# A new order for the first thirty microseconds of an mLSTM and two-layer feed-forward kernel

## The chip, the cores and the metric

The kernel runs on one core of a Trainium2 chip. The metric is the device time of one execution in microseconds (us), the median of several runs.

## The reference, cut to what matters

An mLSTM over 2 batches, 8 heads, 768 steps and 40 features per head gives 1536 rows of 320 numbers; two feed-forward layers follow (widths 768 and 2048).

```python
for t in range(S):
    m_new = np.maximum(f_gate[:, :, t] + m, i_gate[:, :, t])
    f_stab = np.exp(f_gate[:, :, t] + m - m_new)
    i_stab = np.exp(i_gate[:, :, t] - m_new)
    C = f_stab * C + i_stab * outer(v_t, k_t)
    n = f_stab * n + i_stab * k_t
    y[:, :, t] = sigmoid(o_t) * (C @ q_t) / max(abs(n . q_t), 1)
x = y as (B*S, H*D)
h = maximum(maximum(x @ w1, x @ w2), x @ w3); x = h @ w_out
h = x @ w_in; g = h * tanh(softplus(h)); out = g @ w_out2
```

## The kernel before, in words

The sequence is cut into 6 chunks of 128 steps; with 2 batches that makes 12 units, u = 0 to 11. Units 0 and 1 are the first chunk of each batch, units 2 and 3 the second. The three products of the first layer are made in blocks of 512 rows, and the first block needs units 0 to 3 whole. So the beginning of the kernel is: gates, units 0 to 3, and then the first products.

The order of the work is written out by hand in PLAN (lines 31 to 65), a list of words. Each word is the name of a step, its arguments and, behind an @, the PSUM banks that it uses. follow (L660) goes through the words, and under manual_schedule (L671) each engine's queue gets its instructions in the order of the words. PE, DVE, ACT, POOL and SP have one queue each and work through it strictly in order; SP issues all transfers. Between engines only the data and the reuse of buffers and banks make one wait for the other. So a word that is moved changes its place on its own engine's queue and leaves the other queues as they were.

The words that matter here, with their engine and line:

- SP: first:0 to first:3 (L186) load the gates of the first chunk, the other gates, the identity idt and a mask; lq:u (L300, two transfers) loads queries and keys of a unit into qall, which has two buffers; ln:u (L305) loads na (values, keys, output gate of a unit, two buffers); l3:u (L310) another layout of the queries; out:c (L290, L294, L295) writes decays to DRAM, and lc:u (L330, three transfers) reads them back as broadcasts, cp; fet:w,g (L494) fetches group g of the nine groups of first-layer weights, with three buffers.
- DVE: ma (L191, L195), fa:0, ia:0, fl:0 and ca (L283) are the gates' scans; D:u,j (L346) makes half of a unit's decay matrix out of PSUM; X:u,j (L365) multiplies the scores into it; den (L405 to L407), xn (L418) and sg:2, sg:3 (L412) divide and gate; mg:w,g (L509) puts weights together.
- ACT: fe, ie (L210 to L217, L241, L243) are exponentials, pick (L267) and eye (L271) copy parts of idt, fl:1 (L224), gc (L260, L263), dl (L154), G (L386, a sigmoid), sc:w,g (L503, L504, two passes over a fetched weight group), rd (L154), C:0, C:1 (L478), sd (L468), xc (L154), xh (L441, L445). Changing between exponential and sigmoid costs a load of ACT's table.
- POOL: clear:4 to clear:7 (L171 to L178), fa, ia, flp (L204, L205, L236, L228), V (L371), K (L381), Q (L376), sg:0, sg:1 (L412), cut:w,g (L549, L551, L552).
- PE: fill:n (L487) makes n matmuls on zeros that nobody reads; F:u,j (L339) broadcasts decays into PSUM; S:u (L359) makes the scores; gt (L252, L255) transposes gates; N (L396, L398) makes a unit's output, O (L460) its state update, T (L429) transposes it; Pa and P (L578) are the products of the first layer.

## Time and profile before

| | us |
|---|---|
| median of 3 runs | 375.26 (375.0 to 375.54) |
| the profiled execution, its own time | 374.55 |
| span of the profiled execution, first to last instruction | 372.8 |
| PE busy in the span | 367.4 |
| DVE, ACT, POOL busy | 198.6, 175.5, 100.1 |
| moved by DMA | 38.80 MB, mean 104 GB/s |

The time lies 1.75 us above the span, which is what stands around the first and the last instruction. Busy time of PE is nearly the whole span, but it tells little of the beginning: there PE is often filled with matmuls that wait in a row behind the slowest of their suppliers.

### The profile page before, as it was taken

The page shows a single profiled execution, that of the slowest core. Times are in us where ns is not written, and L with a number is a line of the kernel's source. Part 1 is how long each engine was busy: PE and PEld are TensorE (multiplying, and loading weights), DVE is VectorE, ACT ScalarE, POOL GpSimd, SP SyncE. Part 2 cuts the span into 40 slices and gives each one's busy share as a digit, 9 for nine tenths or more (in the row PEclk, how much of TensorE's full clock was granted, in tenths as well). Part 3 has the DMA queues.
Part 4 walks back from the last instruction along what each step waited for, and adds up shares of the span by engine and source line. Part 5 has one row for each costly group of instructions (what it writes and reads, how often), then busy time and mean ns, then how long its engine had stood idle before and what let it go on. Part 6 is the DMA issues. An engine that isn't in the chain of part 4 may idle for free.

```text
span 372.8 us, 7435 instructions
## 1 busy us (share of the span) xinstructions
PE 367.4 (99%) x2999; PEld 317.2 (85%) x3000; DVE 198.6 (53%) x344; ACT 175.5 (47%) x353; POOL 100.1 (27%) x111
## 2 busy tenths in 40 slices
PE   8999999999999999999999999999999999999996
PEld 4898888888888898888777889989989989989986
DVE  6989999998556853565581745512212112212112
ACT  4887777933413202555644876543333233333231
POOL 6784575755202022311540052330010110000000
PEclk9999999999999999999999999999999999999999
DMA  7879995938590310033220530000200000200001
GB/s 204 270 248 307 355 283 166 267 100 273 192 316 8 105 55 2 18 123 110 103 70 2 223 131 3 3 2 0 72 2 2 2 0 2 72 2 3 2 0 70
DMA packets 15668, 38.80 MB, mean 104 GB/s; under 512 B 1886, under 2 KB 8515, under 8 KB 15635
## 3 DMA queue, kind: packets, MB, share of 16 engines
q1 hardware_dynamic: 15635, 38.34, 31.3%
q8 instruction: 23, 0.38, 0.4%
q14 instruction: 10, 0.08, 0.1%
HBM read 36.29 MB, written 2.04 MB: 103 GB/s over the span
## 4 chain that ended last, share of the span: by engine, by line
PE 90%; DVE 3%; DMA 3%; ACT 1%; issue 1%; SPq 1%; DVEq 0%; ACTq 0%
PE mm L578 24%; PE o L719 23%; PE h L719 22%; PE it L398 4%; PE sc_c L359 2%; PE mz L621 2%; PE mz L620 2%; PE mz L622 2%; PE it L396 2%; DMA qall<-in_qk_dram 2%; PE mz L625 1%; PE mz L626 1%; PE sp L460 1%; DMA idt<-in_ident_dram 1%; PE xp L429 1%
## 5 line engine op out<-in xcount | busy, mean ns | idle before, releaser
L748 DVE TENSOR_TENSOR gl<-g,gh 128x512 fp32r<-128x512 f32 x48 | 34.8, 729 | 102.0 <-ACT g L747 102.0
L719 PE MATMUL o<-wo,gh 64*128 64x320 f32 (+1 forms) x736 | 85.0, 306 | 0.0
L719 PE MATMUL h<-zh,wi 64*128 64x512 f32 x480 | 75.2, 390 | 0.0
L578 PE MATMUL mm<-xh,w 128*128 128x512 f32 x270 | 72.0, 396 | 0.0
L719 PEld LDWEIGHTS o<-wo,gh 64*128 64x128 f32 (+1 forms) x736 | 65.1, 185 | 2.2 <-issue 0.4
L746 ACT ACTIVATE gh<-h 128x512 fp32r<-128x512 f32 x48 | 29.0, 604 | 77.8 <-PE h L719 77.6
L719 PE MATMUL o<-wo,gl 64*128 64x320 f32 (+1 forms) x368 | 59.3, 306 | 0.0
L578 PEld LDWEIGHTS mm<-xh,w 128*128 128x128 f32 x270 | 49.4, 188 | 10.7 <-issue 0.4
L719 PEld LDWEIGHTS h<-zh,wi 64*128 64x128 f32 x480 | 44.1, 185 | 9.3 <-ACT zraw L633 0.5
L719 PE MATMUL h<-zl,wi 64*128 64x512 f32 x240 | 47.3, 391 | 0.0
L578 PE MATMUL mm<-xl,w 128*128 128x512 f32 x162 | 45.7, 390 | 0.1
L578 PEld LDWEIGHTS mm<-xl,w 128*128 128x128 f32 x162 | 30.3, 188 | 6.9 <-issue 0.5
L719 PEld LDWEIGHTS o<-wo,gl 64*128 64x128 f32 (+1 forms) x368 | 36.1, 185 | 0.0
L596 DVE TENSOR_TENSOR zraw<-zraw,mm 128x512 f32<-128x512 f32 x36 | 24.6, 682 | 20.7 <-PE mm L578 19.1
L747 ACT ACTIVATE g<-h 128x512 f32<-128x512 f32 x48 | 29.2, 608 | 0.0
L719 PEld LDWEIGHTS h<-zl,wi 64*128 64x128 f32 x240 | 22.5, 184 | 5.3 <-issue 0.4
L658 POOL TENSOR_TENSOR zl<-zraw,zh 128x512 fp32r<-128x512 f32 x9 | 11.6, 1291 | 54.9 <-ACT zh L652 54.8
L606 POOL TENSOR_TENSOR hl<-zraw,hh 128x512 fp32r<-128x512 f32 x11 | 15.3, 1388 | 39.1 <-DVE hh L152 24.0
L398 PE MATMUL it<-vp,dt 128*128 128x41 f32 x192 | 25.2, 272 | 0.2 <-DVE dt L365 0.2
L398 PEld LDWEIGHTS it<-vp,dt 128*128 128x128 f32 x192 | 24.1, 192 | 0.5 <-DVE dt L365 0.3
L594 ACT ACTIVATE zraw<-mm 128x512 f32<-128x512 f32 x18 | 10.7, 592 | 21.8 <-PE mm L578 21.7
L346 DVE TENSOR_TENSOR_SCAN dt<-dt,eye 128x512 f32<-128x512 f32 x16 | 19.1, 1206 | 0.0
(153 smaller groups left out, 523.0 us busy)
## 6 DMA issues: line engine op xcount, KB each, us to landing
na<-in_nat_dram SPq DMA_DIRECT2D x12, 484.0 KB
raw_w<-in_w_dram SPq DMA_DIRECT2D x9, 640.0 KB
raw_i<-in_wi_dram SPq DMA_DIRECT2D x8, 640.0 KB
raw_p<-in_wo_dram SPq DMA_DIRECT2D x8, 640.0 KB
dt<-dram_f SPq DMA_DIRECT2D x8, 512.0 KB
qall<-in_qk_dram SPq DMA_DIRECT2D x24, 160.0 KB
raw_o<-in_wo_dram SPq DMA_DIRECT2D x3, 640.0 KB
out_dram<-ob SPq DMA_DIRECT2D x12, 160.0 KB
```

The lines of the kernel that those rows point to most:

```text
L346: nc.vector.tensor_tensor_scan(half, *((t["fp", j], idr) if ("fp", j) in t else (half, eyes[0])), 0.0, op0=ALU.mult, op1=ALU.add)
L359: nc.tensor.matmul(scs[h % 2][:, (h // 2) * L:(h // 2 + 1) * L], qk[r:r + 64, 1, h // 2], qk[r:r + 64, 0, h // 2], start=True, stop=True)
L398: nc.tensor.matmul(it[:, h], t["dt"][:, h], vps[u % 2][:, h], start=(c == 0), stop=(c == 0 or h == h1 - 1))
L578: nc.tensor.matmul(ups[blk, m, i], *seq[k], start=(k == 0), stop=(k == 7))
L594: nc.scalar.activation(top(blk, m), ups[blk, m, 0], AF.Copy)
L596: nc.vector.tensor_tensor(top(blk, m), top(blk, m), ups[blk, m, i], op=ALU.max)
L606: engine(dve).tensor_tensor(ls, top(blk, m), h.bitcast(F32), op=ALU.subtract)
L658: nc.gpsimd.tensor_tensor(zl[:, j], zraw[:, j, t0:t0 + tb], zh[:, j].bitcast(F32), op=ALU.subtract)
L719: mm = nc.tensor.matmul(out_, a, r, start=first, stop=last).ins
L746: mark[blk, m] = nc.scalar.activation(gh, ps, AF.Mish)
L747: nc.scalar.activation(g, ps, AF.Mish)
L748: low[blk, m] = nc.vector.tensor_tensor(gl, g, gh.bitcast(F32), op=ALU.subtract)
```

## The change

Only the first six lines of PLAN are written anew (a part of them, up to the word T:1); the steps themselves and all words behind stay. There are 146 words in the changed lines, before and after.

```diff
-    "tables: clear:4 first:0 clear:1 clear:2 clear:0 clear:3 fill:9@m1 first:1 clear:5 ln:0 first:2 lq:0 fet:w,0 ma:0 lq:1 l3:2 fa:0 fill:2@m0 ma:1 fe:0 fill:4@c1 "
-    "fa:1 ia:0 fl:0 ie:0 pick: gt:0@c1 ma:2 clear:6 fe:1 F:0,1@m2 F:1,1@m0 eye: F:0,0@c0 ca:1 clear:7 F:1,0@s1 fl:1 D:0,1 ia:1 out:1 flp:1 ie:1 fa:2 ln:1 "
-    "gt:1@s0 D:1,1 first:3 gc:1 gc:0 S:0@m2,s0 fet:w,1 sc:w,0 D:1,0 V:0 lc:2 F:2,1@m1 D:0,0 F:3,1@s2 lq:2 G:0 mg:w,0 F:2,0@c1 dl:0 X:0,0 K:0 rd:w,0,1 "
-    "S:1@m0,s1 fill:7@c0 G:1 X:0,1 ia:2 ln:2 dl:1 l3:3 rd:w,0,0 D:2,1 N:0 lq:3 V:1 X:1,1 cut:w,0,1 lc:3 fe:2 X:1,0 F:3,0@m1 K:1 O:0@m2 den:0 ie:2 O:1@c0 D:2,0 sg:0 "
-    "S:2@s1,m0 Q:2 C:1 xn:0 D:3,1 dl:2 N:1 ln:3 C:0 V:2 fet:w,2 lq:4 cut:w,0,0 xc:0 X:2,0 X:2,1 T:0@c1 K:2 S:3@s2,c0 den:1 G:2 D:3,0 sc:w,1 Q:3 N:2@m0 ca:2 "
-    "dl:3 xh:0 X:3,0 V:3 out:2 O:2@m1 X:3,1 sd:2 sg:1 l3:4 out:0 den:2 K:3 N:3@s2 xn:1 fet:w,3 sc:w,2 sg:2,1 mg:w,1 xn:2 xc:1 lc:4 G:3 T:1 den:3 xc:2 "
+    "tables: clear:4 first:0 first:1 clear:1 clear:2 clear:0 clear:3 fill:8@m1 first:2 clear:5 clear:7 clear:6 lq:0 ln:0 ma:0 lq:1 ln:1 fa:0 ma:1 fe:0 "
+    "pick: eye: fa:1 ia:0 fl:0 fe:1 ie:0 F:0,1@m2 fill:2@m1 ma:2 ia:1 F:0,0@c0 ca:1 fl:1 D:0,1 out:1 flp:1 ie:1 F:1,1@m0 D:0,0 S:0@s0,s2 first:3 lq:2 l3:2 fa:2 "
+    "gt:0@c1 F:1,0@s1 gc:0 dl:0 D:1,1 gt:1@c1 gc:1 ia:2 F:2,1@m1 D:1,0 fe:2 ie:2 F:3,1@m2 V:0 F:2,0@c1 lc:2 X:0,0 dl:1 G:0 X:0,1 K:0 fill:4@c0 S:1@m0,s1 lq:3 ln:2 G:1 "
+    "D:2,1 N:0 l3:3 V:1 X:1,1 X:1,0 K:1 fet:w,0 lc:3 O:0@s2 den:0 C:0 F:3,0@m1 sg:0 fill:2@c0 D:2,0 dl:2 S:2@s1,m0 xn:0 O:1@c0 xc:0 C:1 fet:w,1 Q:2 N:1 "
+    "D:3,1 ln:3 V:2 lq:4 G:2 X:2,0 X:2,1 T:0@c1 K:2 S:3@s2,c0 den:1 sc:w,0 D:3,0 Q:3 N:2@m0 "
+    "dl:3 xh:0 X:3,0 V:3 O:2@m1 fet:w,2 X:3,1 mg:w,0 sd:2 rd:w,0,1 ca:2 cut:w,0,1 rd:w,0,0 sc:w,1 sg:1 l3:4 out:0 out:2 den:2 K:3 N:3@s2 cut:w,0,0 xn:1 fet:w,3 sc:w,2 sg:2,1 mg:w,1 xn:2 xc:1 lc:4 G:3 T:1 den:3 xc:2 "
```

Sorted by queue, the two orders read so where they differ:

- SP before: first:0, first:1, ln:0, first:2, lq:0, fet:w,0, lq:1, l3:2, out:1, ln:1, first:3, fet:w,1, lc:2, lq:2, ln:2, l3:3, lq:3, lc:3, ln:3, fet:w,2, lq:4, out:2, l3:4, out:0, fet:w,3.
- SP after: first:0, first:1, first:2, lq:0, ln:0, lq:1, ln:1, out:1, first:3, lq:2, l3:2, lc:2, lq:3, ln:2, l3:3, fet:w,0, lc:3, fet:w,1, ln:3, lq:4, fet:w,2, l3:4, out:0, out:2, fet:w,3.
- PE before: fill:9, fill:2, fill:4, gt:0, F:0,1, F:1,1, F:0,0, F:1,0, gt:1, S:0, F:2,1, F:3,1, F:2,0, S:1, fill:7, N:0, F:3,0, O:0, O:1, S:2, N:1, and on.
- PE after: fill:8, F:0,1, fill:2, F:0,0, F:1,1, S:0, gt:0, F:1,0, gt:1, F:2,1, F:3,1, F:2,0, fill:4, S:1, N:0, O:0, F:3,0, fill:2, S:2, O:1, N:1, and on as before.
- DVE: D:0,0 comes second instead of fourth; mg:w,0 and ca:2 move behind X:3,1.
- ACT: pick and eye come right behind fe:0; fe:2 and ie:2 come before G:0 and G:1; sc:w,0 and rd:w,0 move behind G:2 and sd:2.
- POOL: clear:7 and clear:6 come before fa:1, ia:2 before V:0; cut:w,0,1 stands between V:3 and sg:1, cut:w,0,0 behind K:3.

Of the kernel before, what the change touches and what calls it, by code (L numbers as in the profile page):

```python
# [15 lines left out]
B, H, S, D = 2, 8, 768, 40  # L16
# [12 lines left out]
ZAT = (5, 12, 13)  # L29
LATE = {4: "i7", 6: "p4", 8: "p5", 10: "p6", 12: "p7"}  # L30
PLAN = (
# [882 lines left out]
```

## Rows read from the trace of the kernel before

**Rows 1.** One piece of the chain that ended last: start, length, what.

```profile
34.78 13.65 PE mm L578 x59
```

**Rows 2.** Busy time by stretch: PE, PEld, DVE, ACT, POOL, then granted clock, DMA share, GB/s.

```profile
0.00:2.00 2.00, 0.61 (x2) 0.28 (x3) 1.04 (x5) 1.27 (x1) 1.42 (x6) 1.00 0.03 8
2.00:9.00 7.00, 6.89 (x26) 3.17 (x25) 4.71 (x11) 2.67 (x11) 4.37 (x11) 1.00 0.90 255
12.00:14.00 2.00, 2.00 (x25) 1.75 (x24) 2.00 (x3) 1.61 (x4) 0.48 (x1) 1.00 0.90 336
14.00:16.00 2.00, 1.95 (x13) 1.32 (x12) 2.00 (x3) 1.93 (x6) 2.00 (x3) 1.00 0.59 200
23.00:27.00 4.00, 4.00 (x41) 3.88 (x42) 3.53 (x6) 2.95 (x9) 3.45 (x4) 1.00 0.71 274
372.00:372.80 0.80, 0.00 (x0) 0.00 (x0) 0.00 (x0) 0.00 (x0) 0.00 (x0) 0.57 0.00 0
```

**Rows 3.** DMA issues by tensor: number of transfers in the whole kernel, KB of each.

```profile
na<-in_nat_dram SPq DMA_DIRECT2D x12, 484.0 KB
raw_w<-in_w_dram SPq DMA_DIRECT2D x9, 640.0 KB
...
qall<-in_qk_dram SPq DMA_DIRECT2D x24, 160.0 KB
...
cp<-dram_c SPq DMA_DIRECT2D x30, 60.0 KB
```

**Rows 4.** Timeline of PE: start, length, line, count, [idle before, releaser].

```profile
1.39 6.11 PE L487 MATMUL fill<-zraw 128*128 128x512 bf16 x15 [1.39 <-DVE zraw L162]
...
22.94 0.34 PE L359 MATMUL sc_c<-qall 64*128 64x128 f32 x1 [0.16 <-DMA qall<-in_qk_dram]
...
29.56 0.53 PE L429 MATMUL xp<-idt,xn 128*128 128x128 f32 x3
...
31.62 0.68 PE L429 MATMUL xp<-idt,xn 128*128 128x128 f32 x3
...
33.31 0.96 PE L578 MATMUL mm<-xh,w 128*128 128x512 f32 x3
```

**Rows 5.** Timeline of DVE.

```profile
4.75 1.38 DVE L195 TENSOR_TENSOR_SCAN scr<-scr 16x512 f32<-16x512 f32 x1
6.95 0.42 DVE L283 TENSOR_TENSOR_SCAN scr<-scr 16x128 f32<-16x128 f32 x1 [0.83 <-POOL scr L236]
8.51 4.57 DVE L346 TENSOR_TENSOR_SCAN dt<-fp,idr 128x512 f32<-128x512 f32 x4 [1.14 <-PE fp L339]
12.99 0.80 DVE L509 SCALAR_TENSOR_TENSOR dec_w<-dec_w,raw_w 128x640 int32<-128x640 int32 x1
...
27.20 0.48 DVE L418 TENSOR_TENSOR xn<-it,sg 128x320 f32<-128x320 f32 x1
...
29.77 0.17 DVE L405 TENSOR_SCALAR den<-it 128x8 f32<-128x8 f32 x1 [0.45 <-PE it L398]
...
30.47 0.49 DVE L412 TENSOR_TENSOR sg<-sg,den 128x320 f32<-128x320 f32 x1
```

**Rows 6.** Timeline of ACT.

```profile
5.97 0.21 ACT L267 ACTIVATE sel<-idt 128x16 fp32r<-128x16 f32 x1 [1.31 <-DMA idt<-in_ident_dram]
...
11.57 1.28 ACT L386 ACT_TABLE_LOAD   x1
...
26.96 0.80 ACT L503 ACTIVATE dec_w<-raw_w 128x640 f32<-128x640 f32 x1 [0.33 <-DMA raw_w<-in_w_dram]
...
28.48 0.47 ACT L386 ACTIVATE sg<-na 128x320 f32<-128x320 f32 x1
```

**Rows 7.** Timeline of POOL.

```profile
4.12 0.44 POOL L204 TENSOR_TENSOR scr<-scr 16x128 f32<-16x128 f32 x1 [1.76 <-DVE scr L195]
...
16.20 0.45 POOL L551 TENSOR_TENSOR w<-dec_w,w 64x128 fp32r<-64x128 f32 x1
...
25.74 0.73 POOL L371 TENSOR_TENSOR vp<-na,gTr 128x328 f32<-128x328 f32 x1
```

## The prediction, made before the change was run

> **What bounds the kernel now.** I read the chain that ended last first. From the start of the first-layer products it is PE alone: 59 matmuls in a row, 13.65 us [rows 1]. The time is therefore settled by when those products begin (33.31 [rows 4]); an earlier or later start moves everything behind it by as much, as long as weights arrive in time. So I asked who sets 33.31, and took the engines' timelines one after the other. The reader is to see two kinds of waits. Early on, DVE waits for PE before the first of its four long scans [rows 5], and ACT waits 1.31 us for idt, the table that the first broadcast needs [rows 6]: these are waits that an order of work can shorten. Later, PE waits for the scores' data of unit 3 at 22.94 [rows 4] and ACT waits for the third weight group at 26.96 [rows 6]: these are transfers. The table by stretch says the same: the DMA engines are 0.90 busy from 2 us on [rows 2]. There are thus two limits side by side, the work of DVE and PE and the bytes, and the change touches both.
>
> **The change part by part.**
>
> Fills: nine, two and four become eight and two ahead of the first broadcasts, so five go. Fifteen took 6.11 us [rows 4], 0.41 each, and eight end at 1.39 + 3.26 = 4.65 instead of 7.5. The first broadcast no longer stands behind fifteen of them. The fills before S:1 shrink from seven to four, and two go before S:2, which waits for DVE there; these six cover waits and I cost them at nothing (0.8 us at most for the two, and less than the idle time that PE has before N:3, below).
>
> idt goes ahead of ln:0 in SP's queue. It landed just before 5.97 [rows 6], with the 484 KB of na [rows 3] ahead; at 255 GB/s [rows 2] those take 1.94 us, so it lands at about 4.0. The values na come later by 80 KB of idt and 320 KB of lq:0, but nobody reads them before the first V, far behind. With pick right behind fe:0, the first broadcast can run at about 4.75, when the DVE scan that follows fl:0 begins [rows 5].
>
> POOL: the clears go into the 1.76 us in which POOL idled before fa:1 [rows 7]; should they not fit wholly, fa:1 is late by the rest, some tenths, which ma:2's scan on DVE covers. fa:1 starts at 4.12 and takes two operations of 0.44, so fe:1 can start at 5.0. From pick to ca:1, with fe:1 between, was 0.98 us (5.97 to 6.95), so ca:1 is ready by 6.0. It then waits for ma:2, which ends at 6.13, takes 0.42, and the four scans start at 6.55 in place of 8.51 [rows 5]: 2.0 us earlier. mg:w,0 (0.80) leaves the row of work behind them [rows 5], so the scores of units 0 and 1 are multiplied in 2.8 us earlier. On ACT, exponentials ahead of the sigmoids save two loads of the table, 1.28 each [rows 6], which are beside the path. gt and S change places and banks on PE; S:0 comes before gt:0, gc:0 and gc:1, which only V waits for.
>
> If that were all, the products would begin 2 to 2.8 us earlier. But the transfers: what stands on the queue ahead of na of unit 3 is the same list of transfers in both orders; it is only sorted otherwise. Those of unit 3's scores landed at 22.94 [rows 4], the third weight group at 26.96 [rows 6]; between them lie cp (3 x 60 KB), na (484) and the weights (640) [rows 3]. Shared out by bytes, na of unit 3 lands at 22.94 + 664/1304 x 4.02 = 25.0, before and after. The third weight group now also stands behind lq:4, two times 160 KB [rows 3]. That transfer costs 0.98 us at 336 GB/s and 1.64 at 200 [rows 2]. I take 0.98, since in the new order SP issues well ahead of the transfers, as in the stretch with 336. The weights thus land at 26.96 + 0.98 = 27.94.
>
> What waits for these two? *First*, POOL's queue: V:3 at 25.0, and behind it now two cuts of 0.45 each [rows 7], then sg:1. V:3 to xn:1 took 27.20 - 25.74 = 1.46 [rows 5, 7], so xn:1 starts at 25.0 + 1.46 + 0.9 = 27.4, which is 0.2 later than before. From there to sg:3 it was 3.27 us, of which 0.45 were a wait for N:3 [rows 5]; N:3 starts right behind V:3 now and ends earlier, so sg:3 can be at 27.4 + 2.82 = 30.2. *Second*, ACT's queue: sc:w,2 waits for the weights, and behind it stand xc:1, G:3 and xc:2. From sc:w,2's start to the end of G:3 was 28.95 - 26.96 = 1.99 us [rows 6], so G:3 ends at 29.9 and lets sg:3 start at 30.2, against 30.47 [rows 5]. xc:1, just ahead of G:3, ends at about 29.6. The last third of T:1 waits for it; from the start of T:1 to T:3 lay 2.06 us (29.56 to 31.62 [rows 4]), less 0.2 for the two thirds that are done by then, so T:3 starts at 31.45 in place of 31.62: 0.17 earlier, and the first product with it. The first weight group stands 1304 KB ahead of na's end (cp, the second group, na), which at 274 GB/s [rows 2] puts it near 20; sc:w,0 and mg:w,0 then have 13 us to the first product and hold up nothing.
>
> Sum: 374.55 (the profiled execution) less 0.2 is 374.35; the median of the runs stands 0.71 above that execution, so 375.26 - 0.2 = **375.1**. The 2.8 us of the start turn into idle time of PE and DVE before N:3 and T:1. A measurement of this kernel can tell about 0.2% (0.75 us) from no change, so this is no change.
>
> **The rivals.**
>
> *The transfers land earlier (B).* The DMA engines were only 0.71 busy from 23 to 27 us and 0.59 from 14 to 16 [rows 2]; part of this was SP waiting with transfers in hand. If the new order fills 1.16 us of it (0.29 x 4), both gates come that much earlier, and T:3 too: 375.1 - 1.1 = 374.0. At most the compute limit is left, 2.0 us: 373.3. Against it: loads in many small pieces (cp) may be slow in any order.
>
> *The queue runs dry (C, slower).* Before, the first two weight groups filled the DMA engines while lq:2 and lq:3 waited for S:0 and S:1. Now only 1784 KB stand ahead of lq:2 (gates and idt 176, twice 320 of scores' data, twice 484 of na), which at 255 GB/s [rows 2] are through at 2.0 + 7.2 = 9.2 us. S:0 stands behind ten fills and three broadcasts, near 9 (an estimate). A transfer that is issued to an empty queue takes more than 1 us to flow: in the first 2 us the DMA engines are 0.03 busy [rows 2], though loads head SP's queue. So up to 1.2 us of DMA time is lost there, and both gates come later by it: 376.3. It decides from the point at which S:0 ends later than about 8.
>
> *lq:4 is dear (E).* At 200 GB/s it costs 1.64, the weights land at 28.6, and the time is 375.1 + 0.66 = 375.8. The Trainium skill (DMA: Bandwidth & Descriptors, Why a DMA increments its semaphore by 16 and not by 1) says that a transfer is spread over the largest number of engines up to 16 that divides its outer dimension, so the 40 rows of these loads would take ten engines of sixteen. By that rule the price would be 1.6 times that of 336 GB/s, 1.56 us, and the sum 375.6; no row of this case shows single engines.
>
> *The clock falls (D, slower).* PE gets idle gaps of over 1 us before N:3 and T:1 that it did not have. At the end of the span, with no PE work in it, the granted clock's mean over 0.8 us is 0.57 [rows 2], part of it at 1.2 GHz. Were it to fall in these gaps, the products would start at half speed; at the price of the opening (6.11 us of fills, where half the time is 3 us), 378. For most of that time PE has some work, so I give it little.
>
> **How the numbers follow.** A 0.40, B 0.30, E 0.12, C 0.13, D 0.05. B is faster by over 0.2%, C and D slower, A and E mostly the same; A's and E's own spread gives 0.03 to faster and 0.02 to slower. So faster 0.33, same 0.47, slower 0.20. The range takes in A, E, C and most of B, 373.4 to 376.4, and leaves out D and B's far end.
>
> **What would show it.** Right: D:0,1 near 6.6; DVE 2.5 us ahead at den:0; then a wait of POOL's V:3 for na until about 25 and of ACT's sc:w,2 for raw_w until about 28; PE idle before N:3 and before T:1's end; the first product within 0.5 us of 33.3. Wrong: V:3 and sc:w,2 without a wait, or landings before 24 and 27 (B); a DMA share under 0.7 between 9 and 14 us (C); a granted clock below 1 between 23 and 40 us (D). The forecast also falls if the products, once started, stop for weights.

## The result, and the profile after

The changed kernel takes 379.58 us in the median of 6 executions (378.65 to 381.21), the kernel before, run beside it, 375.24 (374.42 to 379.27): a ratio of 1.0104, 95% interval 1.0056 to 1.0151. The forecast was 375.1, with a range that ended at 376.4. The change is slower by 4.3 us, some six times the 0.75 us that the prediction gives as the least that a measurement can tell. The profiled execution has a span of 377.9 (before 372.8) and a mean granted clock of 0.985. On the chips of the experiments 38 of 70 executions of the kernel before had a mean granted clock of 0.97 to 0.98 and took 381 to 386 us, longer than five of the six of the kernel after; the ratios below, but not the medians, leave these out, and one long execution of e11 and two of e12 with them.

The chain that ended last, from the 6.66 of the first write to the products (start, length, what):

```profile
6.66 5.12 DMA dram_c<-scr
...
13.39 3.99 DMA qall<-in_qk_dram
...
17.45 8.67 DMA na<-in_nat_dram
...
28.43 0.72 POOL sg L412
29.15 0.68 POOL kp L381
29.83 1.48 POOL w L549
31.31 0.02 issue
31.34 0.79 ACT dec_w L503
...
38.71 6.46 PE mm L578 x27
```

The products begin 5.33 us later (38.64 in the timeline below, against 33.31 [rows 4]), and the span grew by 5.1. Behind the first product nothing has changed: 377.9 - 38.64 = 339.3, before 372.8 - 33.31 = 339.5. So the loss lies in the first 39 us, and the chain names its links: a write, two loads, POOL's steps from V:3 to the cut L549, then ACT.

The timelines of the four engines in the kernel after: first PE, then DVE, ACT and POOL (start, length, line, count, idle before and its releaser).

```profile
27.35 0.86 PE L398 MATMUL it<-vp,dt 128*128 128x41 f32 x6 [2.33 <-POOL vp L371]
...
32.98 0.48 PE L429 MATMUL xp<-idt,xn 128*128 128x128 f32 x1 [1.84 <-ACT xn L154]
...
35.85 0.85 PE L429 MATMUL xp<-idt,xn 128*128 128x128 f32 x3
38.64 1.53 PE L578 MATMUL mm<-xh,w 128*128 128x512 f32 x5
...
6.67 4.57 DVE L346 TENSOR_TENSOR_SCAN dt<-fp,idr 128x512 f32<-128x512 f32 x4
...
29.18 0.49 DVE L418 TENSOR_TENSOR xn<-it,sg 128x320 f32<-128x320 f32 x1 [1.79 <-POOL sg L412]
...
33.32 0.49 DVE L412 TENSOR_TENSOR sg<-sg,den 128x320 f32<-128x320 f32 x1 [0.42 <-ACT sg L386]
...
4.25 0.20 ACT L267 ACTIVATE sel<-idt 128x16 fp32r<-128x16 f32 x1
...
21.90 0.78 ACT L503 ACTIVATE dec_w<-raw_w 128x640 f32<-128x640 f32 x1 [2.50 <-DMA raw_w<-in_w_dram]
...
26.75 0.76 ACT L503 ACTIVATE dec_w<-raw_w 128x640 f32<-128x640 f32 x1
...
31.34 0.79 ACT L503 ACTIVATE dec_w<-raw_w 128x640 f32<-128x640 f32 x1 [3.16 <-POOL w L549]
...
26.28 1.01 POOL L371 TENSOR_TENSOR vp<-na,gTr 128x328 f32<-128x328 f32 x1 [1.80 <-ACT w L154]
27.37 0.45 POOL L551 TENSOR_TENSOR w<-dec_w,w 64x128 fp32r<-64x128 f32 x1
...
29.79 1.51 POOL L549 TENSOR_TENSOR w<-dec_w,w 128x512 fp32r<-128x512 f32 x1
```

The early part came as forecast: the first step of pick (sel) at 4.25 (5.97 before [rows 6]) and the four scans at 6.67 (8.51 before [rows 5]). Then the gain is lost in three places. V:3, the step for which the rows na of unit 3 are loaded, starts at 26.28 (25.74 [rows 7]); in the chain the rows land at 17.45 + 8.67 = 26.12. sc:w,2, the third ACT L503, starts at 31.34 (26.96 [rows 6]) and no longer waits for its weights but for POOL: L549 is cut:w,0,0. In the kernel before, this cut was done by 22.66:

```profile
21.38 1.28 POOL L549 TENSOR_TENSOR w<-dec_w,w 128x512 fp32r<-128x512 f32 x1
```

And from the last third of T:1 (32.98) to the first product it takes 5.66 us, where it was some 3.5 (29.56 plus 0.2 for the first two thirds, to 33.31 [rows 4]).

Busy time by stretch, kernel after (PE, PEld, DVE, ACT, POOL, then granted clock, DMA share, GB/s), and below three stretches of the kernel before:

```profile
2.00:10.00 8.00, 8.00 (x54) 5.43 (x53) 7.61 (x13) 3.67 (x15) 7.30 (x13) 1.00 0.83 219
10.00:16.00 6.00, 5.95 (x52) 4.80 (x54) 5.93 (x11) 4.36 (x11) 3.99 (x6) 1.00 0.68 195
16.00:23.00 7.00, 7.00 (x76) 6.59 (x76) 4.62 (x9) 2.88 (x8) 2.47 (x4) 1.00 1.04 303
25.00:27.00 2.00, 0.02 (x1) 0.00 (x0) 1.90 (x4) 1.44 (x5) 0.72 (x1) 1.00 0.76 268
27.00:28.60 1.60, 1.25 (x12) 1.25 (x12) 0.36 (x2) 1.18 (x2) 1.37 (x4) 1.00 0.60 216
28.60:38.90 10.30, 8.46 (x47) 7.25 (x47) 7.94 (x17) 5.72 (x16) 5.66 (x6) 0.50 0.81 286
38.90:60.00 21.10, 21.10 (x112) 17.53 (x113) 18.42 (x26) 15.65 (x33) 14.10 (x18) 1.00 0.80 272
```

```profile
2.00:10.00 8.00, 7.89 (x33) 4.07 (x32) 5.71 (x12) 2.74 (x12) 5.29 (x12) 1.00 0.91 257
10.00:16.00 6.00, 5.95 (x57) 4.91 (x58) 6.00 (x7) 5.53 (x13) 3.76 (x5) 1.00 0.82 256
16.00:23.00 7.00, 6.84 (x67) 6.28 (x65) 6.46 (x15) 6.37 (x16) 5.70 (x9) 1.00 0.92 264
```

Two things stand here. From 2 to 10 us the transfers ran at 219 GB/s in place of 257 and from 10 to 16 at 195 in place of 256: 38 x 8 + 61 x 6 = 670 KB less, of which 39 x 7 = 273 KB were made up by 23 us. The 397 KB that stay missing are 1.3 us at 303 GB/s. And the granted clock is 0.50, the lower level of 1.2 GHz, from 28.6 to 38.9 us, after two microseconds (25 to 27) in which PE was busy for 0.02.

### The profile page after: what moved, and what is told of

Same layout as the page of the kernel before. It is cut to its first block, busy times and chain, and to the rows that moved or that the text cites. A ratio compares the mean times of both kernels' runs of the same rounds, so it can differ in the third digit from the quotient of the medians.

```text
span 377.9 us, 7416 instructions
## 1 busy us (share of the span) xinstructions
PE 368.4 (97%) x2993; PEld 319.2 (84%) x2994; DVE 199.1 (53%) x344; ACT 173.1 (46%) x351; POOL 101.4 (27%) x111
## 4 chain that ended last, share of the span: by engine, by line
PE 87%; DMA 5%; DVE 4%; ACT 1%; POOL 1%; issue 1%; SPq 0%; DVEq 0%; POOLq 0%; ACTq 0%
PE mm L578 24%; PE o L719 22%; PE h L719 22%; PE it L398 3%; DMA na<-in_nat_dram 2%; PE sc_c L359 2%; PE mz L621 2%; PE mz L620 2%; PE mz L622 2%; PE it L396 1%; DMA dram_c<-scr 1%; PE xp L429 1%; PE sp L460 1%; PE mz L625 1%; PE mz L626 1%; DMA qall<-in_qk_dram 1%
## 5 line engine op out<-in xcount | busy, mean ns | idle before, releaser
L398 PE MATMUL it<-vp,dt 128*128 128x41 f32 x192 | 26.0, 277 | 2.5 <-POOL vp L371 2.3
```

The source lines that it names most:

```text
L398: nc.tensor.matmul(it[:, h], t["dt"][:, h], vps[u % 2][:, h], start=(c == 0), stop=(c == 0 or h == h1 - 1))
```

## The experiments

Three theories came out of these rows: **buffer** (dec, the scaled weights, has two buffers at L499, so sc:w,2 must wait until group 0 is cut, and the change put that cut behind unit 3's steps on POOL), **clock** (it fell in PE's wait), **transfers** (the queue ran dry, so that unit 3's rows are late). The table holds all kernels that gave a comparable time; the median is in us, the ratio is to the kernel before on the same chip, and the last four columns are of the one profiled execution. Time before, the median behind each ratio: 375.2 to 375.6 on every chip. The kernel after itself was not timed beside the experiments.

| run | median (n) | ratio, 95% interval | V:3 | sc:w,2 | first product | span |
|---|---|---|---|---|---|---|
| after | 379.58 (6) | 1.0104, 1.0056 to 1.0151 | 26.28 | 31.34 | 38.64 | 377.9 |
| e1_fills | 377.67 (6) | 1.0061, 1.0032 to 1.0090 | 27.27 | 32.05 | 37.21 | 376.3 |
| e2_cut_dve | 378.00 (10) | 1.0082, 1.0049 to 1.0114 | 25.74 | 30.14 | 36.74 | 375.9 |
| e3_fet_early | 379.79 (4) | 1.0122, 1.0066 to 1.0178 | 25.93 | 30.71 | 38.04 | 377.9 |
| e4_all | 377.68 (6) | 1.0073, 1.0044 to 1.0101 | 27.19 | 30.49 | 36.89 | 376.1 |
| e5_fills_cut | 376.76 (6) | 1.0062, 1.0024 to 1.0100 | 27.40 | 30.94 | 36.18 | 375.4 |
| e6_queues | 376.65 (10) | 1.0056, 0.9999 to 1.0114 | 26.66 | 31.37 | 35.13 | 374.3 |
| e7_unit3_first | 376.43 (6) | 1.0040, 1.0008 to 1.0072 | 23.07 | 33.88 | 33.31 | 373.4 |
| e8_sp_before | 386.32 (4) | 1.0309, 1.0175 to 1.0444 | 27.24 | 35.62 | 42.72 | 381.9 |
| e9_tuned | 380.21 (6) | 1.0136, 1.0074 to 1.0198 | 25.67 | 40.65 | 37.32 | 379.6 |
| e10_rows_first | 379.59 (4) | 1.0124, 1.0069 to 1.0178 | 25.83 | 32.99 | 40.29 | 379.8 |
| e11_unit3_fill | 378.14 (4) | 1.0123, 1.0025 to 1.0221 | 22.45 | 34.76 | 34.16 | 375.1 |
| e12_unit3_clock | 375.68 (12) | 1.0010, 0.9995 to 1.0026 | 24.97 | 34.86 | 34.29 | 374.3 |
| e14_rows_before_w1 | 376.03 (11) | 1.0021, 1.0007 to 1.0035 | 26.21 | 32.95 | 36.70 | 375.9 |

Read the last two columns first: span less first product is 339.1 to 339.5 in before, after, e1, e2, e4, e5, e6, e8, e10 and e14. One number, the first product, carries nearly every difference. It is more in e3 (339.9), e12 (340.0), e7 (340.1), e11 (340.9) and e9 (342.3); e7 and e12 show a stall of 0.57 us behind the start of the products.

**Clock alone.** Matmuls on zeros on both sides of N:3, where PE waited:

```diff
-"... out:2 den:2 K:3 N:3@s2 cut:w,0,0 xn:1 ..."
+"... out:2 fill:14@s1 den:2 K:3 N:3@s2 fill:14@s1 cut:w,0,0 xn:1 ..."
```

> Kernel after, with 14 matmuls on zeros on PE ahead of N:3 and 14 behind it, in the two stretches in which PE idled (24.0 to 27.3 and 30 to 33 us); nothing else is moved. Clock theory (the fall of the granted clock at 28.7 us costs time of its own): the clock stays 1.00 from 8 to 45 us, the piece from T:1's last third to the first product shrinks from 5.7 us to about 3.5, and the time is 2.1 us less than 379.6: 377.5. Rival (the first product is late by its suppliers alone, PE's rate does not matter): the time stays at 379.6 within 0.5. Landing of na of unit 3 (26.1) and start of sc:w,2 (31.3) stay in both.

Measured 377.67, as in the clock theory. Stretches of that run, same columns:

```profile
24.00:27.00 3.00, 3.00 (x18) 1.45 (x17) 2.97 (x4) 2.44 (x8) 1.00 (x1) 1.00 0.98 325
27.00:30.00 3.00, 2.52 (x22) 2.31 (x20) 0.89 (x5) 1.69 (x3) 2.50 (x5) 1.00 0.76 210
30.00:38.00 8.00, 7.86 (x58) 5.16 (x57) 7.33 (x16) 5.33 (x14) 4.59 (x5) 1.00 0.64 236
```

With PE kept busy the clock stays at its upper level of 2.4 GHz, and from sc:w,2 to the first product it takes 37.21 - 32.05 = 5.16 us, where it was 38.64 - 31.34 = 7.30. Those 2.1 us are the clock, although this execution's V:3 and sc:w,2 were later than in the kernel after. All six executions had a mean clock of 0.998 or more and took 377.21 to 378.33; the six of the kernel after had 0.981 to 0.986 and took 378.65 to 381.21, and e3, on the chip of e1, 378.56 to 380.37. So no execution overlaps, though the intervals of the ratios do.

**Buffer alone.** The cut of group 0 goes to DVE (the fourth argument):

```diff
-"... N:3@s2 cut:w,0,0 xn:1 ..."
+"... N:3@s2 cut:w,0,0,1 xn:1 ..."
```

> Kernel after, with cut:w,0,0 on DVE instead of POOL. Buffer theory (sc:w,2 waits for cut:w,0,0, which reads the older of the two dec buffers, and that cut stands on POOL behind V:3, the first cuts, sg:1 and K:3): sc:w,2 starts near 28.2 in place of 31.34, T:3 comes 1.2 to 2.6 us earlier, and the time is about 377.3 (377.0 to 378.4). Rival (the third weight group's own landing, forecast near 28, or the late na of unit 3 holds the chain): sc:w,2 may start earlier, but the first product and the time move by less than 0.5 us: above 379.0.

378.00. ACT's row shows that the wait changed its owner:

```profile
30.14 0.79 ACT L503 ACTIVATE dec_w<-raw_w 128x640 f32<-128x640 f32 x1 [3.25 <-DMA raw_w<-in_w_dram]
```

sc:w,2 starts 1.2 us earlier and now waits for the weights. The buffer is a real wait, and right behind it stands the next one. Of the 1.2 us, 0.54 are this execution's earlier V:3 (25.74): with the cut on POOL, sc:w,2 started 5.06 us behind V:3 in the kernel after and 4.78 in e1 and e3, which would be 30.5 to 30.8 here. So the move by itself gained 0.4 to 0.7 us at sc:w,2 (an estimate from these executions); the 1.6 us by the medians are compared across chips.

**Transfers, a first form.** fet:w,0 ahead of lc:2, so that the queue has something to move while SP waits for the write of out:1:

```diff
-"... lc:2 X:0,0 ..."   "... K:1 fet:w,0 lc:3 ..."
+"... fet:w,0 lc:2 X:0,0 ..."   "... K:1 lc:3 ..."
```

> Kernel after, with fet:w,0 issued ahead of lc:2 instead of behind l3:3, that is in the stretch from 12 to 16 us in which the DMA engines ran half empty. Transfer theory (na of unit 3 is late because DMA time was lost while SP waited for the write of dram_c): the first weight group is moved in the empty time, na of unit 3 lands near 24 in place of 26.1, V:3 and all behind it come 2 us earlier, 377.5, and less (375.5) should the clock stay up because PE's gaps shrink. Rival (the queue was not really empty, the sum of the bytes sets the landing): na of unit 3 lands within 0.5 us of 26.1 and the time stays above 379.0.

379.79: nothing. V:3 waits until 25.93, 0.35 us less.

```profile
2.00:10.00 8.00, 8.00 (x52) 5.42 (x50) 7.58 (x13) 3.68 (x15) 7.28 (x13) 1.00 0.81 243
10.00:16.00 6.00, 6.00 (x56) 4.80 (x55) 5.93 (x11) 4.33 (x11) 3.97 (x6) 1.00 0.91 267
16.00:23.00 7.00, 7.00 (x75) 6.59 (x75) 5.28 (x11) 3.95 (x13) 2.98 (x5) 1.00 0.94 266
```

By 23 us this kernel had moved 8 x 243 + 6 x 267 + 7 x 266 = 5.41 MB, the kernel before 5.44 and the kernel after 5.04. So the missing bytes were made up, and the rows were still late: the bytes alone do not set their landing. This form of the theory falls.

**All three mends** (the cut on DVE, the early fetch, ten fills ahead of N:3):

> Kernel after with all three: fet:w,0 ahead of lc:2, cut:w,0,0 on DVE, and ten matmuls on zeros ahead of N:3. If the three causes together explain the loss, the first product begins at 32.5 to 33.5 (33.31 before, 38.64 after) at full clock and the time is 374.3 to 375.4, no slower than the kernel before. Rival (a fourth cause remains): above 376.5.

377.68, far from the forecast of 374.3 to 375.4 and in the rival's range: a further cause is open. sc:w,2 again waits for its weights, until 30.49.

**Clock and buffer together** (fills of 14 and 10 around N:3, cut:w,0,0 on DVE):

> The changed kernel with matmuls on zeros ahead of and behind N:3 and with cut:w,0,0 on VectorE: the two causes mended that the earlier runs priced singly (1.9 us for the clock, 1.6 us for the buffer). Theory (the prices add, and nothing else is late): first product at 35.4 or earlier, granted clock 1.00 throughout, 376.1 (375.6 to 376.8). Rival (a third wait takes over, the landing of the third group of weights at 29 to 30, which holds ScalarE's sc:w,2 and the steps queued behind it): sc:w,2 at 29.5 to 30.5 waiting for a DMA, first product at 36 or later, 377.0 to 378.

376.76, the first product at 36.18, sc:w,2 at 30.94. The time is at the far end of the theory's range and the first product later than it said. The profile names no load before sc:w,2, but all cuts of group 0 had ended by 29.59 (the one on DVE by 28.75), so that only the weights are left: the rival's order of waits, not its time. The ten fills behind N:3 (30.61 to 32.78 in the chain that ended last) stand right ahead of T:1 (32.83), so they may cost some tenths themselves. The two prices (1.9 and 1.6 us by the medians) give 2.8 together.

**The queues too** (as e5, but with six fills behind N:3 in place of ten; sc:w,2 behind xc:2 on ACT, sg:1 ahead of cut:w,0,1 on POOL):

```diff
-"... sc:w,1 sg:1 ... cut:w,0,1 ... sc:w,2 sg:2,1 mg:w,1 xn:2 ... den:3 xc:2 "
+"... sc:w,1 sg:1 cut:w,0,1 ... sg:2,1 mg:w,1 xn:2 ... den:3 xc:2 sc:w,2 "
```

> As the run before, and sc:w,2 is moved behind xc:2 on ScalarE, sg:1 ahead of cut:w,0,1 on GpSimd, so that no step of units 1 and 2 stands behind a wait for weights. Theory (ScalarE's queue is what the late weights cost): T:1 to T:3 no longer wait for the third group, first product at 33 to 34, 375.0 (374.3 to 376). Rival (the first product waits for unit 3's rows, which are late by themselves, not for the weights): first product and time within 0.4 us of the run with the two mends.

376.65 and the first product at 35.13. The time is the rival's; the first product came 1.05 us earlier than in e5, where the rival allowed 0.4 and the theory wanted 33 to 34, and four fills fewer are a part of the edit. The chain that ended last begins with the late rows and V:3 at 26.66 and still holds sc:w,2 (31.37), now ahead of xc:3 on ACT.

**Unit 3's rows ahead of all weights**, and group 0 scaled, merged and cut behind the steps of units 2 and 3:

```diff
-"... K:1 fet:w,0 lc:3 ..."   "D:3,1 ln:3 V:2 ... den:1 sc:w,0 D:3,0 ..."
+"... K:1 ln:3 lc:3 fet:w,0 ..."   "D:3,1 V:2 ... den:1 D:3,0 ..."
-"... X:3,1 mg:w,0 sd:2 rd:w,0,1 ca:2 cut:w,0,1 rd:w,0,0 sc:w,1 sg:1 ... cut:w,0,0 xn:1 fet:w,3 sc:w,2 sg:2,1 mg:w,1 xn:2 xc:1 ..."
+"... X:3,1 ca:2 sg:1 ... xn:1 sd:2 xc:1 ... sg:2,1 sc:w,0 xn:2 mg:w,0 rd:w,0,0,1 xc:2 sc:w,1 cut:w,0,0 rd:w,0,1 T:1 den:3 cut:w,0,1 ..."
```

(mg:w,1 stands behind xl:1, sc:w,2 and mg:w,2 behind xl:3.)

> The changed kernel with unit 3's rows (ln:3) ahead of lc:3 and of the first weights on the transfer queue, and the first group of weights scaled, merged and cut behind the steps of units 2 and 3. Theory (what the change lost, it lost because the queue ran dry ahead of unit 3's rows): the rows land at about 21 in place of 26.1, V:3 starts by 22, TensorE has no idle stretch of 2 us, granted clock 1.00, first product at 30 to 32, 373 (372 to 374.5), ahead of both kernels. Rival (the weights become the last arrival: the first product stalls for the first group's cuts, or its later ones): first product at 30 to 32 and stalls behind it, 375 or more.

376.43, its one execution at a full clock 375.15. PE's timeline:

```profile
31.61 0.68 PE L429 MATMUL xp<-idt,xn 128*128 128x128 f32 x3 [2.46 <-DVE xn L418]
...
33.31 1.46 PE L578 MATMUL mm<-xh,w 128*128 128x512 f32 x5
...
37.86 1.39 PE L578 MATMUL mm<-xh,w 128*128 128x512 f32 x5 [0.57 <-DVE st L480]
```

V:3 moved to 23.07 and the first product to 33.31, the very time of the kernel before [rows 4]. Both theory and rival wanted 30 to 32, and the theory's 373 was missed: a gap of 2.46 us ahead of T:3 stayed. On DVE mg:w,0 (27.98) stands ahead of unit 3's den (29.18), and sg:3 takes 1.15 us in place of 0.49 beside the cut on POOL (29.34, 1.26 us long).

**The old order of transfers under the new order of engines:**

```diff
-"... lc:2 X:0,0 ... S:1@m0,s1 lq:3 ln:2 G:1 ..."
+"... fet:w,1 X:0,0 ... S:1@m0,s1 lc:2 lq:2 G:1 ..."
```

(and all other words of SP where the kernel before has them)

> The changed kernel with its transfers issued in the order of the kernel before, all else as changed. Theory (order of the transfers sets the landing of unit 3's rows): they land at about 24.8, V:3 starts at 24.9 to 25.8, the third scaling of weights by 30, 378.0 (376 to 378.6), less where the clock stays up. Rival (the order of transfers does not matter, what moved on the engines does): 379.6 (378.9 to 380.4) with V:3 at 26.0 or later.

386.32, outside both. PE shows why: the new order needs unit 2's queries early, and the old queue brings them late; behind this wait the granted clock is 0.50 from 23 to 27 us.

```profile
19.98 0.46 PE L359 MATMUL sc_s<-qall 64*128 64x128 f32 x2 [3.00 <-DMA qall<-in_qk_dram]
```

So the two halves of the change cannot be priced apart by this run: the new order of the engines does worse with the old order of transfers than with its own.

**A tuned version of e7** (den, sg, xn of unit 3 ahead of all merging, xl:0 and S:4 in idle time, groups 1 and 2 later):

```diff
-"... xn:1 sd:2 xc:1 ... sg:2,1 sc:w,0 xn:2 mg:w,0 rd:w,0,0,1 xc:2 sc:w,1 cut:w,0,0 rd:w,0,1 T:1 den:3 ..."
+"... xn:1 sd:2 sc:w,0 xc:1 ... xl:0 N:3@s2 sg:2,1 xn:2 mg:w,0 xc:2 T:1 den:3 rd:w,0,0 cut:w,0,0 rd:w,0,1 ..."
-"... O:3@m2 xn:3 xl:1 mg:w,1 C:2 xc:3 ... S:4@c0,s1 ..."
+"... O:3@m2 S:4@c0,s1 xn:3 xl:1 xc:3 sc:w,1 C:2 ... mg:w,1 ..."
```

> The run with unit 3's rows first, with its own gap closed: on VectorE the steps of units 2 and 3 (den, sg, xn) run ahead of all merging of weights, on GpSimd xl:0 moves ahead into idle time, the scores of unit 4 (S:4) run in TensorE's gap ahead of T:3, and the second and third groups of weights are scaled and merged after unit 3's steps. Theory (with the rows at 21 the beginning is bounded by unit 3's chain of norms alone, and the first group of weights is ready beside it): first product at 30.5 to 31.5 in place of 33.3, no stall of over 0.5 us behind it, clock 1.00, 373.3 (372.3 to 374.5), ahead of both kernels. Rival (the weights' steps, now later, become the bound): products begin by 31.5 but stall for the cuts of the first or second group, 375 or more.

380.21, a plain miss. In this profiled execution the same order of transfers as in e7 brought everything some 2 us later, and the clock fell:

```profile
24.72 0.99 POOL L376 TENSOR_TENSOR cb<-cp,q 120x384 f32<-120x384 f32 x1 [2.40 <-DMA cp<-dram_c]
25.67 0.73 POOL L371 TENSOR_TENSOR vp<-na,gTr 128x328 f32<-128x328 f32 x1
```

Its one execution with a clock of 0.999 took 377.35, so the clock is not all of it; behind the first product, too, it lost time (342.3). What the order costs by itself stays open.

**The rows first, alone** (ln:3 ahead of fet:w,0, lc:3 and fet:w,1, nothing else):

> The changed kernel with one transfer moved: unit 3's rows (ln:3) ahead of the first weights and of lc:3, nothing else. Theory (the late rows are one of the causes, with a price of their own): rows land at 21 to 22, V:3 starts by 24.5 in place of 26.3, first product at 36.5 to 37.5, 378.0 (377.0 to 378.9). Rival (the steps behind the rows wait for others anyhow, the weights above all, which now land later): the rows land early, the first product stays at 38 or later, 379.3 or more.

379.59: the rival. The first weights now land at 24.4, and ACT, whose queue has sc:w,0 ahead of dl:3, waits for them. V:3 does not get the gain either (25.83, where 24.5 was forecast): Q:3, ahead of it on POOL, waits for cp, whose loads stand behind the rows now.

```profile
24.37 0.79 ACT L503 ACTIVATE dec_w<-raw_w 128x640 f32<-128x640 f32 x1 [4.46 <-DMA raw_w<-in_w_dram]
...
24.87 1.00 POOL L376 TENSOR_TENSOR cb<-cp,q 120x384 f32<-120x384 f32 x1 [4.04 <-DMA cp<-dram_c]
```

**e7 with ten matmuls on zeros in the gap, on bank s1, and mg:w,2 behind C:3:**

> The run with unit 3's rows first, with ten matmuls on zeros in the 2.5 us gap of TensorE ahead of T:3, and with the merge of the third group of weights behind C:3, which held up a bank by 0.6 us. Theory (five of its six runs had a granted clock of 0.985 to 0.995 and were about 1.2 us longer than the one at 1.00, and the gap is where the clock fell): clock 0.998 or more in every run, 374.9 (374.3 to 375.6). Rival (the spread has another cause): clock as before in some runs, 375.8 to 376.8.

378.14, outside both ranges: bank s1 was still being read, so the fills waited and pushed T:3 to 32.65 (31.61 in e7). The longest execution, 382.71, had a clock of 1.000, so not every long one is the clock.

```profile
30.49 2.32 PE L487 MATMUL fill<-zraw 128*128 128x512 bf16 x9 [1.64 <-ACT xr L445]
```

**e7 with ten matmuls on zeros on a free bank:**

```diff
-"... O:3@m2 xn:3 ..."
+"... O:3@m2 fill:10@m0 xn:3 ..."
```

> The run with unit 3's rows first, and only ten matmuls on zeros added in TensorE's gap ahead of T:3, on the bank of unit 2's N step, which is read by then (the bank chosen before was read only at 30.5 and pushed T:3 back). Theory (the spread of that kernel was the clock): clock 0.998 or more in every execution, first product at 33.3 to 33.8, 375.3 (374.9 to 375.9), so the loss of the change is given back and no more. Rival (transfers that differ from run to run set the spread): 376 or more at a full clock.

375.68, ratio 1.0010 (0.9995 to 1.0026): no difference from the kernel before, and the time is the theory's, with the first product 0.5 us behind its range. Ten of the twelve executions had a clock of 0.998 or more and took 374.23 to 376.15; two at 0.985 took 380. So the clock makes the large spread here, and ten fills do not always hold it.

```profile
29.92 2.32 PE L487 MATMUL fill<-zraw 128*128 128x512 bf16 x10
32.59 0.68 PE L429 MATMUL xp<-idt,xn 128*128 128x128 f32 x3 [0.35 <-DVE xn L418]
34.29 1.46 PE L578 MATMUL mm<-xh,w 128*128 128x512 f32 x5
```

**The kernel before with the late cut** (cut:w,0,0 moved from behind lq:4 to behind N:3):

> The kernel before, with one step moved as the change moves it: cut:w,0,0 behind unit 3's steps on GpSimd, nothing else. Theory (the scaled group's two buffers couple ScalarE's sc:w,2 to that cut): sc:w,2 starts at 29 or later in place of 26.96 and waits for GpSimd, T:1 and the first product are later by 1 to 2 us, 376.4 (375.8 to 377.4). Rival (the wait is hidden by other work where the clock holds and the rows are early): sc:w,2 late, first product within 0.4 us of 33.3, 375.3 (374.8 to 375.7).

Inconclusive: one execution of four can be compared, 375.8, which lies at the edge between the two. The profiled execution took 383.15, and the cut is not what held it: unit 3's scores waited for their data until 24.4, the granted clock was 0.50 from 25 to 39 us, the cut had ended at 29.95, and sc:w,2 started at 30.91 right behind sd, which had waited for PE. The buffer's price in the kernel before stays open.

**e6 with ln:3 ahead of fet:w,1:**

> The run with the three mends (clock, buffer, queues; 376.65), with unit 3's rows ahead of the second group of weights on the transfer queue. Theory (the 1.3 us that it stands above the kernel before are the rows, which land 1.4 to 1.8 us later there): rows at 24.5 to 25, V:3 1.5 us earlier, first product about 34, 375.3 (374.8 to 376.0). Rival (the second group's landing takes the rows' place): V:3 earlier, time within 0.4 us of 376.65.

376.03, between the theory's 375.3 and the 376.65 of e6, and the intervals of e6 and e14 overlap. Its profiled execution was its longest (377.68) and shows V:3 at 26.21, 0.45 us earlier than in e6 and not 1.5, right behind Q:3, which waited for cp until 25.18. Supported in direction, not shown.

## Why the prediction was wrong, step by step

**Right.** The opening: fills, idt, pick, POOL's clears, ca:1 and the four scans at 6.67 (6.55 forecast). That the time hangs on the first product. That PE would idle before N:3 and before the end of T:1 (2.33 and 1.84 us). The length of the last stage: forecast 33.14 - 27.94 = 5.20 us from sc:w,2 to the first product, measured 5.16 where the clock held (e1).

**The step that failed** is the sentence on the first weight group: "sc:w,0 and mg:w,0 then have 13 us to the first product and hold up nothing." I asked when the products need group 0, and not who else waits for it. sc:w,2 needs a buffer of dec, of which there are two, and so waits for the last cut of group 0; the change moved this cut behind V:3, sg:1 and K:3. sc:w,2 started at 31.34 where I had 27.94. These 3.4 us and 2.1 us of clock are the whole error: 38.64 - 33.14 = 5.5. It is the error of the profiled execution; by the medians it is 379.58 - 375.1 = 4.5, because the sum's 0.71 between execution and median did not come again (379.68 and 379.58).

The 3.4 us hold two mis-sized landings beside the buffer. V:3 was 26.28 - 25.0 = 1.3 us late. Behind V:3 the weights were forecast 2.94 us later (27.94 - 25.0), and in e2, where they alone hold sc:w,2, they come 30.14 - 25.74 = 4.40 later: another 1.5. What is left for the buffer alone is 5.06 - 4.40 = 0.7 us, an estimate from two executions. So the wait that I denied was on the path, but mending it alone uncovers the weights.

**The transfers.** The rows of unit 3 were forecast at 25.0 in either order; V:3 starts at 26.28. The first weight group, forecast near 20, was taken up at 21.90. The sharing-out by bytes took a full queue for granted. Rival C said that it runs dry, at a cost of up to 1.2 us, and got 0.13. Its sign, a DMA share under 0.7 from 9 to 14 us, came (0.64; before, it was 0.95). Its size fits, too (the 1.3 us above), but e3, which made up the bytes and brought V:3 only 0.35 us forward, does not bear out that the lateness of the rows is this loss. C's stated cause, a wait for S:0 until near 9, did not come: S:0 ended at 7.89 (6.73 + 1.16) and lq:2 was issued at 7.91. SP stood at lc:2 until the write of out:1, issued at 6.66, had landed at 11.78. Why the rows land late stays open.

**The clock.** Rival D got 0.05, because PE would have "some work" in its gaps, though the same forecast turned 2.8 us into idle time of PE there. PE had 0.02 us of work in two, and the clock fell 1.3 us after the work had resumed (27.35 to 28.6). The forecast of 3 us for it was of the right size (2.1). The Trainium skill (TensorE: Matmul & The Clock Gate, Part 1) says that the throttled level is the default and that activity releases it; the stretches of after and e1 agree.

**E, lq:4 dear.** The third group's 30.1 in e2 lies beyond even its 28.6. The 4.40 us there between V:3 and the weights lie behind the rows, where lq:4 stands, and E's own price made them 3.6 (28.6 - 25.0). The low price was taken because SP would issue well ahead of the transfers; in the kernel after SP waited 1.0 and 0.9 us at the two loads of lq:4 and 1.4 us at fet:w,2, each time for an earlier load. No row tells what lq:4 itself has of the rest.

**What is shown and what is not.** Shown: the clock's 2.1 us, by e1; the buffer as a wait, by e2; and that rows first, weights later and a held clock together give back the loss (e12 against the kernel after: 1.0010, at most 1.0026, against at least 1.0056). They give back no more than that: no kernel here is faster than the kernel before. Only estimated: how the 3.4 us divide between rows, weights and buffer. Only argued: that the rows' lateness is what stays when clock and buffer are mended. e3 and e10 moved transfers alone and gained nothing; in e10 what went behind became the next wait.

## What to carry to other kernels

When a step moves on a queue, list everyone who waits for it: the consumers of its data and also the producer that needs its buffer next. When work gets done earlier in a part bound by transfers, the time gained can turn into one long wait of TensorE, as it did here, and such a wait can cost the clock of the stage behind it. Matmuls on zeros held it in all six executions of e1 and in ten of twelve of e12; their bank must be free (e11). An order of the engines and an order of transfers are one design (e8, e10): move them together.

## What the runs showed of the hardware

*The same order of transfers lands differently from execution to execution.* e7, e9, e11 and e12 have one order of transfers, and V:3 starts at 23.07, 25.67, 22.45 and 24.97, each time right behind Q:3, which in e9 and e12 waits for cp. Those 3.2 us are more than most changes here are worth, and single profiles must be read with that in mind.

*VectorE and GpSimd slow each other down.* All steps on dec_w from 0 to 60 us, kernel after (duration in ns, least, median, most):

```profile
L509 DVE SCALAR_TENSOR_TENSOR dec_w<-dec_w,raw_w x7: 811/827/1884, 24.7 to 55.7; 128x640 int32<-128x640 int32 x7
```

The one of 1884 ns runs from 30.10, beside the cut on POOL (29.79, 1.51 us long). The Trainium skill (GPSIMD Engine Reference, 1. Specifications) says that GpSimd shares its SBUF interfaces with VectorE instructions that have two SBUF inputs, as this one has; the row agrees, at 2.3 times the median. Two others that begin while POOL works take 1.08 and 1.12 us (35.04 and 55.68). The other way round it is POOL that loses: its V at 45.24 begins while a step L509 runs on DVE (45.13, 0.82 us long) and takes 1.30 us in place of 0.73.

*A load can wait for another that it has nothing to do with.* In the chain of after, SP issues na at 17.45, when a scores transfer ends (13.39 + 3.99 = 17.38). Counted along the queue, that is the transfer eight places ahead, and so it is in e5 (issue 18.62, landing 18.55) and e6 (18.18, 18.11). It reaches the weights too: in after fet:w,2 is issued at 21.89, behind a wait of 1.4 us for a load of weights. Eight places ahead of it stands fet:w,0, whose group ACT takes up at 21.90, though fet:w,2 has a buffer of its own. So an order of transfers also settles when a later one can be issued.

```profile
SPq L494 <- DMA raw_w<-in_w_dram: 1.4, 1, 1.4
...
21.89 0.35 SPq L494 DMA_DIRECT2D raw_w<-in_w_dram  x1
```
